# Decay rows stored straight from the sums, later raw weight loads, sums left in PSUM, and another form of the second activation

## Chip, cores and metric

The kernel runs on one core of one Trainium2 chip. The metric is the device time of one execution in microseconds; for the kernel before the median of three runs is taken.

## The reference

Attention with a decay over 4 x 8 heads (576 positions, 64 wide), then two feed-forward layers over the 2304 x 512 result, the second with a slope per inner channel:

```
log_f  = log(clip(f, 1e-4, 1));  cum = cumsum(log_f)
scores = q k^T / sqrt(D) + cum[:, None] - cum[None, :]     # causal
x      = softmax(scores) v
h  = x @ w_in1;  g = h * clip(h + 3, 0, 6) / 6;                 x = g @ w_out1
h  = x @ w_in2;  g = max(h, 0) + alpha * min(h, 0);             out = g @ w_out2
```

## The kernel before

**Attention.** There are 32 heads in 16 pairs. A pair has nine units: four tiles of 128 queries of the first head, one tile with the 64 last queries of both, four tiles of the second head. At step t the loop at L566 issues for unit t the scores (`stage1`, L353), for unit t-1 the maximum (`maxes`, DVE) and the exponentials (`exps`, ACT), for unit t-5 the transposes and their copies, and some steps after a pair the product with v (`stage3`). The order on every engine is the order of issue; nothing is rescheduled.

A score is the sum of two matmuls: L364 (or L376) with the high parts `q1` and `k1`, and L365 (or L378) with `q2` and `k2`. Rows 0 to 63 of those hold low parts, and rows 64 to 67 the decay: two rows with the high and low part of `cum` and two constant rows. For heads 0 and 1 these four rows are written in SBUF (`aug_consts`, `aug_rows`). All the others read them from two DRAM buffers, `aq_d` and `ak_d`, in `prep_head` (L313, L314). The prologue (L467 to L540) computes `cum`, splits it into `hl`, which is a part of the tile `ak`, copies it on POOL into a tile `aq` of the layout of `aq_d`, with constants set by memsets, and stores both tiles. The SP queue issues nearly all DMAs, in order: L520 stores `ak`, L536 stores `aq`, `load_head` brings the raw q and k of a head (608 KB) and, for every second head, the values (320 KB). `prep_head` and `prep_low` make the high and low parts of a head, mostly on POOL; for head 2 they are issued after unit 3.

**Weights.** They come as 64-bit floats and are converted by hand in slices: `fetch` (L113) loads a raw slice of 512 KB into one of two buffers, then ACT takes the magnitude (m), DVE does floor, shift, join and sign (f, s, j, g), and the sign step issues the next fetch. Names and times of these steps are in tables such as `CONV_ATT` (L46), whose numbers are the units after which a step is issued. The first two fetches are issued after unit 2 (L550).

**Layers.** The tokens are three blocks of 768, the inner channels eight groups of 256; a set is one group with one block, 24 sets a layer. A set's product with the first weights is made of seven products of half size (`product`, L689) in three kinds of PSUM bank: P1, P6, P7 and P4 in A (two banks), P2 in B, P5 and P3 in C (one bank each). ACT copies P1, P6 and P5 to SBUF (`keep`); DVE adds P2, P7 and P3 to these copies (`add`, L707); P4 is used in its bank. Each of the four sums is activated in three steps (`activate`, L654): `first` on ACT, `second` on DVE, `third` splits the result into a high part on ACT (L682) and a low part on POOL (L683). The products with the second weights (`piece`, L719) of the set before are put between, in the order of the strings `SEQ`. In layer two `first` makes relu(-h) (L666) and relu(h) (L668), and `second` adds them with the factor -alpha (L677). The tiles `t` of the activation have three buffers, the tiles `s` of the kept products four.

Of the kernel before, what the change touches and what calls it, by code (L numbers as in the profile page):

```python
# [8 lines left out]
F32 = mybir.dt.float32  # L9
I64 = mybir.dt.int64  # L10
U32 = mybir.dt.uint32
F32R = mybir.dt.float32r
BF16 = mybir.dt.bfloat16
AF = mybir.ActivationFunctionType
ALU = mybir.AluOpType
# [6 lines left out]
def decay_attention_ffn2_kernel(ctx, tc, qk, v, f, wi1, wo1, wi2, wo2, alpha, out):  # L22
    nc = tc.nc
    NHEAD = qk.shape[0]
    S = f.shape[1]
# [20 lines left out]
    CONV_ATT = "m0 15 f0 16 s0 17 j0 18 g0 19 m1 24 f1 25 s1 26 j1 27 g1 28 hb 33 lb 35 S1 42 S3 42 S2 44 S4 44 ha 51 la 53 hc 53 lc 60 hd 60 ld 62 m2 69 f2 70 s2 71 j2 72 g2 73 m3 78 f3 79 s3 80 j3 81 g3 82 ho0 78 lo0 80 ho1 87 lo1 89 wi0 90 wi1 93 wo0 99 wo1 102"  # L46
# [231 lines left out]
    def attention():  # L278
        with ExitStack() as ax:
# [196 lines left out]
            aq = pro.tile([NPP, 4, QW], F32R, name="aq")  # L476
            hl = ak[:, 2:4, :]
            nc.gpsimd.memset(zero, 0.0)

# [17 lines left out]
            nc.sync.dma_start(out=alpha_sb, in_=alpha)  # L497
            aug_consts(0)
# [5 lines left out]
            nc.gpsimd.memset(aq.bitcast(F32)[:, :, 512:640], 0.0)  # L504
            nc.gpsimd.memset(aq.bitcast(F32)[:, 2:4, 0:512], -1.0)
# [9 lines left out]
            for a in range(2):  # L515
                nc.gpsimd.memset(aq.bitcast(F32)[32 * a:32 * a + 32, 2:4, 512 + 64 * a:576 + 64 * a], -1.0)
            aug_rows(1)
            load_head(2)
            for a in range(2):
                nc.sync.dma_start(out=ak_d[a, 0:NP], in_=ak[32 * a:32 * a + NP].bitcast(F32))  # L520
            load_head(3)
            prep_head(1)
            prep_low(1)
# [7 lines left out]
            scaled("P", aq[:, 0:2, 0:512], hl[:, :, 0:512].bitcast(F32))  # L531
            for a in range(2):
                ps, t0 = slice(32 * a, 32 * a + 32), 512 + 64 * a
                scaled("P", aq[ps, 0:2, t0:t0 + TAIL], hl[ps, :, 512:S].bitcast(F32))
            for a in range(2):
                nc.sync.dma_start(out=aq_d[a, 0:NP], in_=aq[32 * a:32 * a + NP].bitcast(F32))  # L536
            nc.gpsimd.tensor_scalar(out=alpha_sb, in0=alpha_sb, scalar1=-1.0, scalar2=None, op0=ALU.mult)
# [9 lines left out]
            def aside(t, *fns):  # L547
                side.setdefault(t, []).extend(fns)

            aside(2, lambda: fetch(0), lambda: fetch(1))  # L550
# [60 lines left out]
    P = {}  # L611
# [39 lines left out]
    def aside(d, fn):  # L651
        behind.setdefault(now[0] + int(d), []).append(fn)

    def activate(s, gt, i, n, h, d):  # L654
# [5 lines left out]
        def first():  # L660
            t = P["tp"].tile([128, NB], F32, tag="t", name="t")
            if ff == 0:
                nc.scalar.activation(out=t, in_=h(), func=AF.Relu, bias=three, scale=1.0)
                hold["g"] = t
                return
            nc.scalar.activation(out=t, in_=h(), func=AF.Relu, scale=-1.0)  # L666
            hold["g"] = g32 = P["tp"].tile([128, NB], F32, tag="t", name="t") if (i, n) == (1, 0) else h()
            nc.scalar.activation(out=g32, in_=h(), func=AF.Relu)  # L668
            hold["t"] = t

        def second():
            g32 = hold["g"]
            if ff == 0:
                nc.vector.scalar_tensor_tensor(out=g32, in0=g32, scalar=6.0, in1=h(), op0=ALU.min, op1=ALU.mult)  # L674
            else:
                m = g * FT + i
                nc.vector.scalar_tensor_tensor(out=g32, in0=hold["t"], scalar=alpha_sb[:, m:m + 1], in1=g32,  # L677
                                               op0=ALU.mult, op1=ALU.add)
# [10 lines left out]
    def product(s, c, gt, k):  # L689
# [17 lines left out]
        def add(k2):  # L707
            nc.vector.tensor_add(out=c[k2], in0=h, in1=c[k2])  # L708
# [194 lines left out]
```

## Time and profile before

| | us |
|---|---|
| median of three runs (lowest, highest) | 1015.56 (1013.59, 1016.53) |
| profiled execution | 1012.13 |
| span in its profile | 1010.3 |
| TensorE busy | 965.5 (96%) |
| DVE busy | 735.9 (73%) |
| ACT busy | 589.1 (58%) |
| POOL busy | 590.0 (58%) |

The profile is of one execution. Attention takes the first 219 us of it or so, layer one runs to about 620 us, layer two to the end. A busy TensorE means that its matmuls follow each other without a gap; what other engines do beside it costs nothing until a matmul waits. The waits, the chain of work that ended last, the timeline and the tables by stretch tell where that is.

### The profile page before, as it was taken

The numbers are of one execution on the slowest core, as the hardware profiler recorded it, in microseconds if no ns is written. First come the engines' busy times: TensorE is split into PE (matmuls) and PEld (weight loads), VectorE is DVE, ScalarE is ACT, GpSimd is POOL, SyncE is SP. The second block draws the span as 40 slices with busy tenths as digits, with TensorE's granted clock in tenths as the row PEclk, the third lists the DMA queues.
The fourth block names the chain that finished last, engine by engine and source line by source line (L and its number), as shares of the span: only waits on it lengthen the run. The fifth ranks groups of instructions, "written<-read, shape, count | busy, mean of one in ns | idle before, by whom it ended". The sixth has DMA issues, their size and how long they took to land.

```text
span 1010.3 us, 15919 instructions
## 1 busy us (share of the span) xinstructions
PE 965.5 (96%) x5488; PEld 859.7 (85%) x5488; DVE 735.9 (73%) x1284; ACT 589.1 (58%) x1444; POOL 590.0 (58%) x577
## 2 busy tenths in 40 slices
PE   4999999999999999999999989999999999999998
PEld 3767666678899999998998988789898888898997
DVE  6888988857698788878989846145687788735454
ACT  5677787776555555555654445665565656564452
POOL 8567568956646666566485269566556556532222
PEclk9999999999999999999999999999999999999999
DMA  6555576501424444310576851332344420243531
GB/s 219 174 173 168 176 239 208 150 2 42 156 66 177 178 175 169 107 48 1 198 308 241 308 184 48 137 129 81 125 160 168 166 84 1 104 182 142 229 150 68
DMA packets 36868, 147.57 MB, mean 146 GB/s; under 512 B 4668, under 2 KB 4668, under 8 KB 33652
## 3 DMA queue, kind: packets, MB, share of 16 engines
q1 hardware_dynamic: 36784, 146.56, 41.7%
q8 instruction: 43, 0.70, 0.3%
q14 instruction: 37, 0.30, 0.1%
q10 hardware_dynamic: 4, 0.00, 0.0%
HBM read 98.26 MB, written 44.14 MB: 141 GB/s over the span
## 4 chain that ended last, share of the span: by engine, by line
PE 57%; DVE 23%; POOL 7%; ACT 6%; issue 4%; DMA 2%; SPq 0%; POOLq 0%; ACTq 0%; DVEq 0%
PE o L733 13%; PE hA L700 12%; PE o L731 12%; PE hC L700 7%; PE pv L454 4%; PE hB L700 3%; DVE nm L341 3%; PE tp L397 2%; DVE t L674 2%; PE sc L364 2%; POOL wi L185 2%; POOL g L683 1%; DVE r L751 1%; DVE s L708 1%; ACT g L682 1%
## 5 line engine op out<-in xcount | busy, mean ns | idle before, releaser
L731 PE MATMUL o<-g,wo 128*128 128x384 f32 x1152 | 233.3, 341 | 2.0 <-POOL g L683 2.0
L700 PE MATMUL hA<-xh,wi 128*128 128x384 f32 x768 | 225.8, 339 | 9.0 <-ACT s L705 5.4
L733 PE MATMUL o<-wo,g 128*128 128x512 f32 x864 | 225.5, 395 | 4.0 <-POOL g L683 3.0
L683 POOL TENSOR_TENSOR g<-t,g 128x384 fp32r<-128x384 f32 x120 | 128.8, 1073 | 156.1 <-ACT g L682 134.6
L731 PEld LDWEIGHTS o<-g,wo 128*128 128x128 f32 x1152 | 205.6, 189 | 4.6 <-POOL g L683 3.3
L733 PEld LDWEIGHTS o<-wo,g 128*128 128x128 f32 x864 | 159.8, 188 | 33.2 <-POOL g L683 6.2
L683 POOL TENSOR_TENSOR g<-s,g 128x384 fp32r<-128x384 f32 x72 | 74.7, 1038 | 155.6 <-ACT g L682 153.8
L700 PEld LDWEIGHTS hA<-xh,wi 128*128 128x128 f32 x768 | 142.0, 188 | 15.1 <-ACT s L705 7.6
L751 DVE TENSOR_TENSOR r<-o,r 128x512 f32<-128x512 f32 x126 | 86.2, 687 | 73.8 <-PE o L733 73.7
L700 PE MATMUL hA<-xl,wi 128*128 128x384 f32 x384 | 129.7, 338 | 0.0
L682 ACT CAST g<-t 128x384 fp32r<-128x384 f32 x120 | 61.9, 515 | 113.0 <-DVE t L674 97.3
L700 PE MATMUL hC<-xh,wi 128*128 128x384 f32 x384 | 115.0, 340 | 3.6 <-ACT s L705 3.6
L740 DVE SCALAR_TENSOR_TENSOR r<-o,r 128x384 f32<-128x384 f32 x168 | 90.6, 549 | 21.2 <-PE o L731 21.0
L349 ACT ACTIVATE p<-sc,nm 128x128 f32<-128x128 f32 (+4 forms) x160 | 84.6, 532 | 22.9 <-DVE nm L341 10.9
L245 POOL TENSOR_TENSOR xl<-r,xh 128x384 fp32r<-128x384 f32 x65 | 78.5, 1225 | 4.1 <-ACT xh L240 3.7
L341 DVE TENSOR_REDUCE nm<-sc 128x1 f32<-128x128 f32 (+4 forms) x160 | 71.7, 470 | 10.1 <-PE sc L366 8.5
L700 PEld LDWEIGHTS hC<-xh,wi 128*128 128x128 f32 x384 | 71.3, 189 | 6.7 <-ACT s L705 4.6
L700 PEld LDWEIGHTS hA<-xl,wi 128*128 128x128 f32 x384 | 72.4, 189 | 3.1
L682 ACT CAST g<-s 128x384 fp32r<-128x384 f32 x72 | 37.1, 515 | 60.1 <-DVE s L677 53.4
L397 PE MATMUL tp<-ident,p 128*128 128x128 f32 x384 | 68.6, 282 | 0.6 <-ACT pt L413 0.6
L364 PE MATMUL sc<-k,q 128*128 128x256 f32 (+2 forms) x128 | 55.6, 434 | 11.9 <-DVE k L332 9.8
L700 PE MATMUL hC<-xl,wi 128*128 128x384 f32 x192 | 65.1, 339 | 0.0
(128 smaller groups left out, 1901.8 us busy)
## 6 DMA issues: line engine op xcount, KB each, us to landing
wid<-wi SPq DMA_DIRECT2D x24, 896.0 KB
wi<-wid SPq DMA_DIRECT2D x12, 1792.0 KB
rqk<-in_qk SPq DMA_DIRECT2D x32, 608.0 KB
raw<-in_wi SPq DMA_DIRECT2D x32, 512.0 KB
raw<-in_wo SPq DMA_DIRECT2D x32, 512.0 KB
wod<-wo SPq DMA_DIRECT2D x24, 512.0 KB
wo<-wod SPq DMA_DIRECT2D x12, 1024.0 KB
vt<-in_v SPq DMA_DIRECT2D x16, 320.0 KB
```

The source lines that it names most:

```text
L245: e.tensor_sub(out=XS[k][1][:, b, c], in0=x, in1=XS[k][0][:, b, c].bitcast(F32))
L341: nc.vector.tensor_reduce(out=nm[:, i:i + 1], in_=src, axis=AX.X, op=ALU.max, negate=True)
L349: nc.scalar.activation(out=pt[:, c0:c0 + cw], in_=src, func=AF.Exp, bias=nm[:, 0:1], scale=1.0, accum_out=dsts[i])
L364: nc.tensor.matmul(out=sc[:, 0:n], lhsT=q1[:, qs], rhs=k1[:, 0:n], start=True, stop=False)
L397: nc.tensor.transpose(tp[:, j, :], pt[:, 128 * j:128 * j + 128], ident)
L682: nc.scalar.copy(out=gt[n][i][:, 0], in_=hold["g"])
L683: nc.gpsimd.tensor_sub(out=gt[n][i][:, 1], in0=hold["g"], in1=gt[n][i][:, 0].bitcast(F32))
L700: nc.tensor.matmul(out=h, lhsT=a, rhs=b[:, x, kc], start=new and kc + e == 0, stop=kc == KH - 1 and e == 2, skip_group_check=not new)
L731: nc.tensor.matmul(out=o[:, 0:NB], lhsT=a[:, cs], rhs=b, start=st, stop=sp)
L733: nc.tensor.matmul(out=o, lhsT=b[:, cs], rhs=a, start=st, stop=sp)
L740: later(0, lambda: nc.vector.scalar_tensor_tensor(out=acc, in0=o[:, 0:NB], scalar=1.0 / 6.0, in1=acc, op0=ALU.mult, op1=ALU.add))
L751: nc.vector.tensor_add(out=acc, in0=o, in1=acc)
```

## The change

- In the prologue the tile `aq` holds the constant rows only and has half the size. It is set by one memset and two small ones at the start, and stored early; two small stores put zeros where `cum` has none. The rows of `cum` go from `hl` to `aq_d` by three stores, which are issued after head 2's load and ahead of the `ak_d` stores. The three scalings on POOL and the two old stores are gone.
- `prep_head(1)` and `prep_low(1)` are issued after the constants `three`, `ident` and `maskj`.
- The first two fetches are issued after units 13 and 18 in place of unit 2, and the conversion steps of the first two slices after units 20 to 30 in place of 15 to 28.
- The sums with P2 and P3 are written to their PSUM bank; ACT and DVE read them there, in both layers. The sum with P7 goes to SBUF as before, since its bank goes on to take P4.
- In layer two `second` computes h + (1 - alpha) relu(-h). The relu(h) on ACT and its tile are gone.

```diff
--- before.py
+++ after.py
@@ -43,7 +43,7 @@
     LM, LE, LT, LV = 1, 2, 5, 5
     RD, SD, PA, PB = 3, 6, 7, 9
     DRAIN = {9 * NP + 3: 2, 9 * NP + 4: 2, 9 * NP + 6: 2, 9 * NP + 7: 2}
-    CONV_ATT = "m0 15 f0 16 s0 17 j0 18 g0 19 m1 24 f1 25 s1 26 j1 27 g1 28 hb 33 lb 35 S1 42 S3 42 S2 44 S4 44 ha 51 la 53 hc 53 lc 60 hd 60 ld 62 m2 69 f2 70 s2 71 j2 72 g2 73 m3 78 f3 79 s3 80 j3 81 g3 82 ho0 78 lo0 80 ho1 87 lo1 89 wi0 90 wi1 93 wo0 99 wo1 102"
+    CONV_ATT = "m0 20 f0 21 s0 22 j0 23 g0 24 m1 26 f1 27 s1 28 j1 29 g1 30 hb 34 lb 35 S1 42 S3 42 S2 44 S4 44 ha 51 la 53 hc 53 lc 60 hd 60 ld 62 m2 69 f2 70 s2 71 j2 72 g2 73 m3 78 f3 79 s3 80 j3 81 g3 82 ho0 78 lo0 80 ho1 87 lo1 89 wi0 90 wi1 93 wo0 99 wo1 102"
     CONV_ATT1 = "m0 108 f0 109 s0 110 j0 111 g0 112 m1 117 f1 118 s1 119 j1 120 g1 121 S1 143 S3 145 S2 146 ha 146 hc 146 hb 147 la 147 lc 147 lb 148 S4 149 hd 149 ld 150 m2 150 f2 151 s2 151 j2 152 g2 153"
     CONV_FIRST = "ho0 2 m3 2 lo0 3 f3 3 s3 4 j3 5 g3 6 ho1 8 lo1 9 wi0 30 wi1 33 wo0 36 wo1 38"
     CONV_A = "m0 0 f0 2 s0 3 j0 4 g0 5 m1 4 f1 6 s1 7 j1 8 g1 9"
@@ -473,9 +473,12 @@
             zero = pro.tile([NPP, S], F32, name="zero")
             cum = pro.tile([NPP, S], F32, name="cum")
             ak = pro.tile([NPP, 4, S], F32R, name="ak")
-            aq = pro.tile([NPP, 4, QW], F32R, name="aq")
+            aq = pro.tile([NPP, 2, QW], F32, name="aq")
             hl = ak[:, 2:4, :]
             nc.gpsimd.memset(zero, 0.0)
+            nc.gpsimd.memset(aq, -1.0)
+            for a in range(2):
+                nc.gpsimd.memset(aq[32 * a:32 * a + 32, :, 576 - 64 * a:640 - 64 * a], 0.0)
 
             def aug_consts(a):
                 o0 = 576 - 64 * a
@@ -495,14 +498,16 @@
 
             load_head(1)
             nc.sync.dma_start(out=alpha_sb, in_=alpha)
+            nc.sync.dma_start(out=aq_d.rearrange("a h r c -> (a h) r c")[:, 2:4], in_=aq)
+            for a in range(2):
+                nc.sync.dma_start(out=aq_d[a, :, 0:2, 576 - 64 * a:640 - 64 * a],
+                                  in_=zero[32 * a:32 * a + 32, 0:128].rearrange("p (r c) -> p r c", r=2))
             aug_consts(0)
             aug_consts(1)
             make_identity(nc, identb)
             nc.gpsimd.memset(maskb, 0.0)
             nc.gpsimd.affine_select(out=maskb, in_=maskb, pattern=[[-1, 128]], compare_op=ALU.is_ge,
                                     fill=-1.0e9, base=0, channel_multiplier=1)
-            nc.gpsimd.memset(aq.bitcast(F32)[:, :, 512:640], 0.0)
-            nc.gpsimd.memset(aq.bitcast(F32)[:, 2:4, 0:512], -1.0)
             nc.gpsimd.memset(ak[:, 0:2, :].bitcast(F32), 1.0)
             nc.vector.tensor_scalar(out=fl, in0=fl, scalar1=1e-4, scalar2=1.0, op0=ALU.max, op1=ALU.min)
             nc.scalar.activation(out=fl, in_=fl, func=AF.Ln)
@@ -512,15 +517,15 @@
             nc.vector.tensor_sub(out=hl[:, 1, :], in0=cum, in1=hl[:, 0, :].bitcast(F32))
             aug_rows(0)
             prep_low(0)
-            for a in range(2):
-                nc.gpsimd.memset(aq.bitcast(F32)[32 * a:32 * a + 32, 2:4, 512 + 64 * a:576 + 64 * a], -1.0)
             aug_rows(1)
             load_head(2)
+            nc.sync.dma_start(out=aq_d.rearrange("a h r c -> (a h) r c")[:, 0:2, 0:512], in_=hl[:, :, 0:512].bitcast(F32))
+            for a in range(2):
+                ps, t0 = slice(32 * a, 32 * a + 32), 512 + 64 * a
+                nc.sync.dma_start(out=aq_d[a, :, 0:2, t0:t0 + TAIL], in_=hl[ps, :, 512:S].bitcast(F32))
             for a in range(2):
                 nc.sync.dma_start(out=ak_d[a, 0:NP], in_=ak[32 * a:32 * a + NP].bitcast(F32))
             load_head(3)
-            prep_head(1)
-            prep_low(1)
             nc.gpsimd.memset(three, 3.0)
             make_identity(nc, ident)
             nc.gpsimd.memset(maskj, 0.0)
@@ -528,13 +533,9 @@
                 nc.gpsimd.affine_select(out=maskj[64 * a:64 * a + 64], in_=maskj[64 * a:64 * a + 64],
                                         pattern=[[-1, TAIL]], compare_op=ALU.is_ge,
                                         fill=-1.0e9, base=0, channel_multiplier=1)
-            scaled("P", aq[:, 0:2, 0:512], hl[:, :, 0:512].bitcast(F32))
-            for a in range(2):
-                ps, t0 = slice(32 * a, 32 * a + 32), 512 + 64 * a
-                scaled("P", aq[ps, 0:2, t0:t0 + TAIL], hl[ps, :, 512:S].bitcast(F32))
-            for a in range(2):
-                nc.sync.dma_start(out=aq_d[a, 0:NP], in_=aq[32 * a:32 * a + NP].bitcast(F32))
-            nc.gpsimd.tensor_scalar(out=alpha_sb, in0=alpha_sb, scalar1=-1.0, scalar2=None, op0=ALU.mult)
+            prep_head(1)
+            prep_low(1)
+            nc.gpsimd.tensor_scalar(out=alpha_sb, in0=alpha_sb, scalar1=-1.0, scalar2=1.0, op0=ALU.mult, op1=ALU.add)
             px.close()
             ptp = ax.enter_context(tc.tile_pool(name="ptp", bufs=3, reuse_waits="tile"))
             rcp = ax.enter_context(tc.tile_pool(name="rcp", bufs=1, reuse_waits="tile"))
@@ -547,7 +548,8 @@
             def aside(t, *fns):
                 side.setdefault(t, []).extend(fns)
 
-            aside(2, lambda: fetch(0), lambda: fetch(1))
+            aside(13, lambda: fetch(0))
+            aside(18, lambda: fetch(1))
             ops = conv_ops(0, 0)
             for name, t in table(CONV_ATT):
                 aside(t, ops[name])
@@ -664,9 +666,7 @@
                 hold["g"] = t
                 return
             nc.scalar.activation(out=t, in_=h(), func=AF.Relu, scale=-1.0)
-            hold["g"] = g32 = P["tp"].tile([128, NB], F32, tag="t", name="t") if (i, n) == (1, 0) else h()
-            nc.scalar.activation(out=g32, in_=h(), func=AF.Relu)
-            hold["t"] = t
+            hold["g"] = t
 
         def second():
             g32 = hold["g"]
@@ -674,7 +674,7 @@
                 nc.vector.scalar_tensor_tensor(out=g32, in0=g32, scalar=6.0, in1=h(), op0=ALU.min, op1=ALU.mult)
             else:
                 m = g * FT + i
-                nc.vector.scalar_tensor_tensor(out=g32, in0=hold["t"], scalar=alpha_sb[:, m:m + 1], in1=g32,
+                nc.vector.scalar_tensor_tensor(out=g32, in0=g32, scalar=alpha_sb[:, m:m + 1], in1=h(),
                                                op0=ALU.mult, op1=ALU.add)
 
         def third():
@@ -705,7 +705,9 @@
             nc.scalar.copy(out=c[k], in_=h)
 
         def add(k2):
-            nc.vector.tensor_add(out=c[k2], in0=h, in1=c[k2])
+            got = h if k != 7 else c[k2]
+            nc.vector.tensor_add(out=got, in0=h, in1=c[k2])
+            c[k2] = got
 
         if k in (1, 6, 5):
             at.setdefault(now[0], []).insert(0, keep)
```

## Rows read from the trace of the kernel before

**Rows 1.** TensorE's waits, whole span: us in total, times, longest.

```profile
PE sc L365 <- DMA k<-ak_d: 3.9, 1, 3.9
```

**Rows 2.** Chain of waits, first 30 us: start us, us, what.

```profile
13.23 1.31 POOL aq L92 x2
...
14.56 5.79 DMA aq_d<-aq
...
20.73 4.20 DMA k<-ak_d
```

**Rows 3.** Timeline, first 30 us: start us, us, engine, line, operation, idle before.

```profile
3.35 1.39 DVE L507 TENSOR_SCALAR fl<-fl 64x576 f32<-64x576 f32 x1 [0.18 <-DMA fl<-in_f]
...
8.51 1.43 SPq L491 DMA_DIRECT2D q<-ak  x2
...
9.10 1.79 POOL L332 TENSOR_TENSOR k<-rqk,k 64x576 fp32r<-64x576 f32 x1
9.65 1.91 DVE L333 SCALAR_TENSOR_TENSOR q<-rqk,q 64x640 fp32r<-64x640 f32 x1
...
11.27 0.40 SPq L295 DMA_DIRECT2D rqk<-in_qk  x1
...
11.66 0.55 PE L365 MATMUL sc<-k,q 68*128 68x256 f32 x1 [1.34 <-DVE q L333]
...
13.26 0.46 SPq L295 DMA_DIRECT2D rqk<-in_qk  x1
...
14.75 0.59 PE L376 MATMUL sc<-k,q 128*128 128x288 f32 x1
...
16.34 2.86 SPq L117 DMA_DIRECT2D raw<-in_wi  x2
...
20.83 0.36 PE L364 MATMUL sc<-k,q 128*128 128x256 f32 x1
```

**Rows 4.** Stretches, length us; PE, PEld, DVE, ACT, POOL busy; clock, DMA share, GB/s.

```profile
12.00:14.00 2.00, 2.00 (x9) 1.58 (x9) 1.45 (x5) 0.95 (x4) 1.80 (x4) 1.00 0.84 207
14.00:16.00 2.00, 2.00 (x8) 1.48 (x8) 1.18 (x2) 1.00 (x4) 1.36 (x5) 1.00 1.11 352
16.00:18.00 2.00, 2.00 (x13) 1.76 (x11) 1.29 (x4) 0.92 (x4) 1.92 (x4) 1.00 0.91 312
18.00:20.00 2.00, 2.00 (x16) 1.77 (x15) 1.50 (x4) 2.00 (x9) 1.79 (x1) 1.00 0.97 241
...
26.00:28.00 2.00, 2.00 (x11) 1.69 (x11) 1.45 (x6) 1.29 (x6) 0.20 (x1) 0.50 0.82 279
```

**Rows 5.** The same view, one pair each, with and without conversion.

```profile
44.00:57.20 13.20, 12.52 (x91) 8.48 (x91) 11.80 (x26) 9.26 (x34) 6.06 (x8) 1.00 0.59 178
81.50:93.00 11.50, 11.20 (x89) 8.14 (x88) 9.52 (x22) 9.11 (x36) 8.01 (x9) 1.00 0.57 166
```

**Rows 6.** DVE by form: busy us, mean ns; last row min/median/max.

```profile
L751 DVE TENSOR_TENSOR r<-o,r 128x512 f32<-128x512 f32 x126 | 86.2, 687 | 73.8 <-PE o L733 73.7
L674 DVE SCALAR_TENSOR_TENSOR t<-t,s 128x384 f32<-128x384 f32 x72 | 51.8, 720 | 10.1 <-ACT t L663 9.9
...
L708 DVE TENSOR_TENSOR s<-hC,s 128x384 f32<-128x384 f32 x48 | 26.6, 553 | 39.2 <-PE hC L700 27.2 <-ACT s L705 11.4 <-issue 0.3
...
L674 DVE SCALAR_TENSOR_TENSOR t<-t,hA 128x384 f32<-128x384 f32 x24 | 13.3, 553 | 13.7 <-ACT t L663 13.7
...
L674 DVE SCALAR_TENSOR_TENSOR t<-t,s x72: 544/552/1498, 222.0 to 610.1; 128x384 f32<-128x384 f32 x72
```

**Rows 7.** ACT by form, columns as in the group before.

```profile
L668 ACT ACTIVATE s<-s 128x384 f32<-128x384 f32 x72 | 37.9, 527 | 2.3
```

**Rows 8.** Timeline of TensorE: first and last standstill in the two layers.

```profile
218.78 0.44 PE L700 MATMUL hA<-xh,wi 128*128 128x384 f32 x1 [0.41 <-ACT s L705]
...
873.26 1.19 PE L733 MATMUL o<-wo,g 128*128 128x512 f32 x4 [0.35 <-POOL g L683]
```

**Rows 9.** Chain of waits, the passage between the layers.

```profile
634.50 3.75 POOL wi L185 x3
```

## Prediction, made before the changed kernel was run

> **What bounds the kernel now.** I read TensorE's waits first. Almost all of the span TensorE is busy, so the only time to win is where it stands still. After its first matmul, one wait stands out: 3.9 us for a DMA that brings the decay rows of head 2 [rows 1]. The chain of waits for the first 30 us tells why [rows 2]: POOL scales the decay rows into `aq` from 13.23 on, the store to `aq_d` takes from 14.56 to 20.35, and only then the load of those rows and of `ak_d` may start; it takes 4.20 us and lands at 24.93. The timeline [rows 3] shows what else stands in that queue: on SP the rows of head 3 (issued 13.26) go ahead of the `aq_d` store, and two raw weight blocks of 512 KB (16.34, 2.86 us of issuing for both) go between the store and the loads that the scores wait for. TensorE had done the first half of unit 9's scores by 21.19 (20.83 plus 0.36) and had nothing else. The clock granted over 26 to 28 us, right after that standstill, is 0.50, the lower of the two levels, against 1.00 before it [rows 4].
>
> Attention then runs in pairs of heads, nine units each: 11.5 us where no weight is converted, 13.2 us where four conversion steps lie on DVE [rows 5]. The two layers are TensorE's: the timeline of TensorE lists 22 matmuls between 218 and 874 us with a standstill in front; the first and the last are shown [rows 8]. They sum to 8.6 us up to 549, 7.2 us in the passage from layer one to two (598 to 640) and 2.8 us from 790 on. That, 18.6 us, is all that the two edits in the layers can win.
>
> **Part 1, the decay rows.** Removed: three POOL operations and the store that waits for them. Added: a store of the constant rows and two small ones of zeros, issued early, then three stores straight from `hl`, before the `ak_d` stores. The early three cost SP an issue of some 0.4 to 0.7 us each (0.40 and 0.46 for a head's load, 1.43 for two row copies [rows 3]); they follow the alpha load and end by about 5.5 us, before SP's next work at 8.51, which waits for `hl` anyway. Their 0.36 MB go behind the first loads and take 1.0 us at the 352 GB/s of 14 to 16 us [rows 4]; I take nothing for it, and if the first loads are not through by 7.5 us, the first rows of heads 0 and 1 come up to 1.0 us later.
>
> The late three are issued from about 12.2 us. When do they land? By their shapes, 608 KB of head 2 and 320 KB of values stand ahead of them, and they bring 295 KB. That is 1.25 MB. The DMAs moved 0.41 MB in 12 to 14 us, 0.70 MB in 14 to 16, and then 312 GB/s [rows 4], so 1.25 MB are through at 16.4. Tested on the old order: 2.20 MB stood up to its `aq_d` store; these rates give 19.9, and it landed at 20.35, 0.45 later. So the new store lands near 17, not 20.35. The loads of head 2's rows are then issued at 17.2 to 17.9, behind the `ak_d` stores and head 3 (2.17 MB in all, through at 19.7 by the same rates). The old loads stood behind 3.24 MB; 2.22 of it had gone by 20 us, the rest takes 3.3 us at 312 GB/s, and they landed at 24.93, 1.6 later. With 0.5 to 1.6 us more, then, the new loads land at 20.2 to 21.3. TensorE wants them at 21.19. I keep 0.3 us of the 3.9 as left over: gain 3.6, bounds 1.0 and 3.9.
>
> What is moved past what: on SP the `ak_d` stores and head 3's load go behind three issues, 1.2 to 2.1 us, so head 3 lands about 1 us later than now. Unit 13 wants it about 4.5 us after unit 9, so there is room of about 1 us; if it is gone, POOL's preparation of head 3 is what is late next. On POOL, head 1's two steps go behind `three`, `ident` and `maskj`, which filled POOL from 10.89 (9.10 plus 1.79) to 13.23, 2.3 us [rows 2, 3]; they would end near 13 us against 10.89, and unit 4's matmuls, the first to ask for them, begin at 14.75. The cover is 1.5 to 2 us.
>
> The same move has a small gain at the opening. DVE's clamp of f took 1.39 us, beside a POOL memset that is not there any more, and its step for q of head 0 took 1.91 us beside POOL's step for head 1, which is now later; TensorE waited 1.34 us for it [rows 3]. Bounds 0 and 1.1 us; I take 0.6, nearer the row of the clamp, because the first rows' DMAs follow the clamp and land only a little before. The lower clock after the standstill goes with it: at most 1.0 us by the row of 26 to 28 us, but other engines had caught up during the standstill and TensorE ran through piled-up work, so I take 0.
>
> **Part 2, the raw weights at units 13 and 18.** 1.05 MB leave the queue at 16.3 us; counted above. Their conversion steps now lie in units 20 to 30. Before, 2, 4 and 2 of the eight DVE steps lay in the pairs of units 9 to 17, 18 to 26 and 27 to 35; now 0, 4 and 4. Two pairs differ by 1.7 us for four steps [rows 5], that is 0.4 us per step where DVE has no room. The pair that loses two steps was catching up and would gain little, the pair that wins two pays up to 0.85: I take 0.5 lost, bounds 0 and 0.85. The loads are ahead of their first use by 7 and 8 units, about 9 us, against about 2 us of transfer each, so their waits are hidden; without that cover ACT would stand for up to 3 us.
>
> Prologue and attention together: 3.6 + 0.6 - 0.5 = 3.7 us gained.
>
> **Part 3, sums left in their banks.** Per set, the sums of P2 and P3 stay in PSUM. The banks B and C are next written ten or more steps later (a step is about 1.1 us), so no matmul waits. Layer one's step after it (L674) is shown in both forms: 720 ns on average with both operands in SBUF, 553 ns with one in PSUM. The SBUF form's median is 552, its longest 1498 [rows 6], so the difference is not the operand but the cases in which it is held up; the PSUM form is never held up so. Two steps per set save 2 x 0.167 = 0.33 us of DVE. It counts only where DVE leads the chain: in layer one roughly 222 to 266, 425 to 475 and 484 to 550 us, 160 us or 10 sets of 15.8 us, as the chain of waits reads there: 3.3 us, of 8.6 us of standstill. Against it stands the addition's write into PSUM, which no row shows. Lower bound: 0, as it reads PSUM already (553 ns). Upper: 134 ns, the distance to the 512-wide addition, 687 [rows 6], the nearest row of a heavier DVE operation on PSUM. I take 50 ns, nearer the lower row since the shape is the same: 2 x 10 x 0.05 = 1.0 lost. Layer one: 2.3 us gained, bounds 0.6 and 3.3.
>
> The Trainium skill (Perfetto Trace Analysis, Optimizing Scalar/DVE Operations) speaks against this edit: it puts DVE's access overhead at about 60 ns on SBUF and about 125 ns on PSUM. By that page the two additions and the two steps of a set would each cost 65 ns more, 10 x 4 x 0.065 = 2.6 us as an estimate. On the reading side the two forms of L674 do not agree with it (552 at the median against 553); the writing side is shown by no run here.
>
> **Part 4, layer two's activation.** One ACT operation goes per product, 96 in all, 527 ns in its frequent form [rows 7]. ACT isn't the bound, but each stood between the sum and DVE's step, so g comes 0.53 us sooner. The six standstills from 790 on are waits for g, between 0.34 and 0.72 us; taking 0.53 off each leaves 0.26 of 2.8. As queues are in order, I take 2.0, bounds 0 and 2.8. In the passage at 598 to 640 POOL's queue leads (a run of 3.75 us of low parts [rows 9]); I take 0 there. What is held longer: `t` (three buffers) now lives until POOL's subtraction, as in layer one.
>
> **Sum.** 3.7 + 2.3 + 2.0 = 8.0 us. The profiled execution took 1012.1 us (span 1010.3), so it would be 1004.1; the median of the runs is 3.4 us higher, 1015.6, and becomes 1007.5.
>
> **Rivals.**
> (a) The standstill comes back in another place: each of the three late stores waits for the one ahead, or head 3 lands so late that its preparation is waited for. For it: SP is one queue, and the margin is under 1 us. Against: the byte count above. It gives part 1 about 1.0 in place of 3.6, a sum of 5.4: 1010.2.
> (b) The write into PSUM takes the layers' gain back: 134 ns per addition leaves 0.6 in layer one, and with DVE slower layer two keeps about 0.5. For it: no row shows such a write. Sum 4.8: 1010.8. The Trainium skill's page named above points here.
> (c) Slower: the three `t` buffers of layer two. The fourth activation of a set takes the buffer of the first; ACT must wait until POOL has subtracted it, four steps (4.9 us) later. Where a run of 3.75 us of weights lies in front [rows 9], with about 1 us for the subtraction the edge of 4.9 is reached, and ACT's next copies, which free TensorE's bank, stand behind it. It decides as soon as POOL is over 1 us late in most sets: 1.2 us in each of 12 sets is 14 us lost, net 1021.5. Against: layer one holds `t` in the same way, and its ACT waits there are for DVE.
> (d) More than forecast: the clock's 1.0, all of the opening and most of layer one's 8.6 us, together 13 us: 1002.6.
> (e) No visible effect: DVE paces attention, so that what TensorE wins at 21 us is waited away by unit 35, and the layers stay: 1014.
>
> **Chances.** Forecast (gain 5.5 to 11) 0.56; (a) 0.13; (b) 0.13; (c) 0.05; (d) 0.07; (e) 0.06. About 0.3% (3 us) is what a measurement of this kernel can tell from no change, so faster means under 1012.5. The forecast, (d) and about two thirds of (a) and (b) make faster 0.80; the rest of these and (e) make same 0.15; (c) 0.05. The range 1001.5 to 1013 holds the forecast, (a), (b) and (d)'s middle; it leaves out (c), (e) and the far end of (d).
>
> **What the profile of after would show.** TensorE's wait for `k<-ak_d` near 21 us under 1 us, and the clock at 1.00 there; the `aq_d` stores landing near 17; unit 35's values about 3.7 us earlier; L674 near 553 ns in two forms of three; L708 into hB and hC under 610 ns; no L668; standstills after 790 under 1 us in sum. I would be wrong if ACT's first operation of layer two waits for POOL, if L708 is near 690, or if POOL's k of head 3 stands in front of TensorE.

## The result, and the profile after

| | before | after |
|---|---|---|
| median, us (lowest to highest of four runs each) | 1014.58 (1012.88 to 1016.53) | 1002.22 (1000.51 to 1004.06) |
| profiled execution, us (span) | 1012.13 (1010.3) | 1002.13 (1000.3) |
| busy, us: TensorE, DVE, ACT, POOL | 965.5, 735.9, 589.1, 590.0 | 961.3, 718.3, 539.6, 583.5 |

The ratio of after to before is 0.9878, with an interval of 0.9851 to 0.9905: 12.4 us faster (9.6 to 15.1). The forecast gain was 8.0. The profiled executions differ by 10.0 only, because the profiled one of before is 2.4 us faster than its median.

Both programs issue the same 5488 matmuls in the same order. So the start of the n-th matmul in the one trace can be set against the start of the n-th in the other, each counted from the start of its span. The difference is what after has won by then, and where it changes, time was won or lost:

| matmuls | start in before, us | won in the stretch, us | won by its end, us |
|---|---|---|---|
| 0 to 240, prologue and scores of the first 29 units | 9.8 to 51.9 | 3.8 | 3.8 |
| 240 to 300 | 51.9 to 61.2 | -3.2 | 0.6 |
| 300 to 1440, rest of attention | 61.2 to 218.0 | 1.2 | 1.8 |
| 1440 to 3360, layer one | 218.0 to 567.6 | 3.6 | 5.4 |
| 3360 to 3840, passage | 567.6 to 667.0 | -0.6 | 4.8 |
| 3840 to the last, layer two | 667.0 to 1006.1 | 5.0 | 9.8 |

**Prologue and attention.** TensorE's waits of after from 10 to 72 us (us in total, times, longest) begin so:

```profile
PE sc L378 <- DMA k<-k: 3.3, 1, 3.3
PE sc L364 <- ACT p L349: 2.4, 1, 2.4
```

The wait for `k<-ak_d` of [rows 1] is not there any more, and two others stand in its place. The timeline of after (columns as in [rows 3]) shows the opening, the stores and the second of the two:

```profile
3.63 0.47 DVE L512 TENSOR_SCALAR fl<-fl 64x576 f32<-64x576 f32 x1 [0.47 <-DMA fl<-in_f]
...
8.65 0.82 DVE L333 SCALAR_TENSOR_TENSOR q<-rqk,q 64x640 fp32r<-64x640 f32 x1
...
9.99 0.55 PE L365 MATMUL sc<-k,q 68*128 68x256 f32 x1 [0.67 <-ACT q L88]
...
11.47 0.69 SPq L522 DMA_DIRECT2D aq_d<-ak  x1
12.20 1.70 SPq L525 DMA_DIRECT2D aq_d<-ak  x2
14.00 1.18 SPq L527 DMA_DIRECT2D ak_d<-ak  x2
...
16.16 1.27 SPq L313 DMA_DIRECT2D q<-aq_d  x1
...
17.88 0.24 SPq L314 DMA_DIRECT2D k<-ak_d  x1
...
18.94 0.27 ACT L408 COPY pt<-tp 128x128 f32<-128x128 f32 x1 [4.08 <-DMA q<-aq_d]
...
19.75 0.52 PE L364 MATMUL sc<-k,q 128*128 128x384 f32 x1 [2.42 <-ACT p L349]
...
21.31 0.73 POOL L92 TENSOR_SCALAR q<-rqk 128x640 fp32r<-128x640 f32 x1 [2.74 <-DMA rqk<-in_qk]
```

The clamp and the step for q are short now (0.47 and 0.82 us against 1.39 and 1.91), and the first product that needs q starts at 9.99, not at 11.66. The three late stores are issued from 11.47 on without a wait between them, and the loads that read them from 16.16 on. But ACT's first copy into `pt` stands for 4.08 us; the exponentials queue behind it, their bank stays full, and TensorE stands 2.42 us before the scores of unit 7. The row above puts ACT's wait down to a load, `q<-aq_d`; the chain of waits of after goes through the last store of `ak_d`, which lands at 18.62 (an experiment below decides between them). Later the chain passes through the copy `k<-k`, which brings half of head 7's k:

```profile
14.77 3.85 DMA ak_d<-ak
...
46.16 7.24 DMA k<-k
...
53.53 0.37 PE sc L378
```

SP's own waits from 36 to 66 us and its timeline say why that copy took so long:

```profile
SPq L117 <- DVE wa L153: 3.6, 1, 3.6
```

```profile
43.75 0.36 SPq L117 DMA_DIRECT2D raw<-in_wo  x1
...
44.87 0.72 SPq L295 DMA_DIRECT2D rqk<-in_qk  x1
45.69 0.38 SPq L300 DMA_DIRECT2D vt<-in_v  x1
46.16 0.47 SPq L326 DMA_DIRECT2D k<-k  x1
```

SP stood 3.6 us for a sign step (L153) that has to free a raw buffer; then a raw slice, a head's rows, its values and, behind them, the copy went out within 2.4 us. The stretches show both standstills, the empty queue and the burst (columns as in [rows 4]):

```profile
18.00:20.00 2.00, 0.25 (x1) 0.25 (x2) 0.00 (x0) 1.06 (x5) 0.57 (x1) 1.00 0.76 248
20.00:22.00 2.00, 2.00 (x9) 1.38 (x8) 0.94 (x2) 1.98 (x9) 0.69 (x1) 0.50 0.93 307
...
42.00:44.00 2.00, 1.96 (x15) 1.18 (x15) 2.00 (x6) 1.48 (x6) 2.00 (x2) 1.00 0.01 4
...
48.00:50.00 2.00, 2.00 (x17) 1.51 (x15) 1.82 (x9) 1.99 (x9) 0.01 (x1) 1.00 1.05 351
50.00:52.00 2.00, 0.21 (x2) 0.00 (x0) 2.00 (x5) 0.67 (x2) 1.56 (x2) 1.00 1.03 244
...
54.00:56.00 2.00, 2.00 (x12) 1.84 (x11) 1.64 (x4) 0.42 (x2) 1.21 (x3) 0.53 0.73 183
```

The DMAs moved 4 GB/s while SP stood and 351 behind it. After each standstill the granted clock is at the lower level, 0.50 and 0.53, as it was after the old one [rows 4].

**The layers.** DVE and ACT by form in after (columns as in [rows 6]; L709, L674 and L677 on DVE, L668 on ACT):

```profile
L709 DVE TENSOR_TENSOR hC<-hC,s 128x384 f32<-128x384 f32 x48 | 27.0, 562 | 41.8 <-PE hC L700 30.9 <-ACT s L705 9.1 <-ACT wa L137 1.1
L709 DVE TENSOR_TENSOR hB<-hB,s 128x384 f32<-128x384 f32 x48 | 26.7, 556 | 2.0 <-PE hB L700 1.3 <-ACT s L705 0.7
...
L674 DVE SCALAR_TENSOR_TENSOR t<-t,s 128x384 f32<-128x384 f32 x24 | 18.6, 776 | 4.1 <-ACT t L665 4.0
...
L674 DVE SCALAR_TENSOR_TENSOR t<-t,hA 128x384 f32<-128x384 f32 x24 | 13.3, 553 | 14.2 <-ACT t L665 14.0
...
L674 DVE SCALAR_TENSOR_TENSOR t<-t,hC 128x384 f32<-128x384 f32 x24 | 13.1, 545 | 1.1 <-ACT t L665 1.0
L674 DVE SCALAR_TENSOR_TENSOR t<-t,hB 128x384 f32<-128x384 f32 x24 | 13.1, 545 | 2.8 <-ACT t L665 2.8
...
L668 ACT ACTIVATE t<-hC 128x384 f32<-128x384 f32 x24 | 11.8, 491 | 39.0 <-DVE hC L709 38.9
```

An addition into the bank takes 562 ns in hC, where the one into SBUF took 553 [rows 6], and 556 in hB, where it took 549. The activation step that reads its sum in a bank takes 545 ns.

In layer two the waits of TensorE's weight loads (PEld) from 640 us on, first of before, then of after, are these:

```profile
PEld o L733 <- POOL g L683: 4.5, 7, 1.2
PEld o L733 <- ACT g L682: 2.0, 4, 0.9
```

```profile
PEld o L735 <- POOL g L683: 0.3, 1, 0.3
```

Before, the loads waited 6.5 us for g; after, 0.3. I had read only the waits of the matmuls [rows 8]. In the passage, the chain of waits of after has these two pieces:

```profile
576.66 8.25 DMA fd<-wa
...
629.69 3.75 POOL wi L185 x3
```

POOL's run of low parts is as long as in [rows 9], and a transfer of 8.25 us through DRAM stands in front. Nothing was won there.

### The profile page after: what moved, and what is told of

Its sections match the earlier page's. It is cut to its first block, busy times and chain, and to the rows that moved or that the text cites. A ratio compares the mean times of both kernels' runs of the same rounds, so it can differ in the third digit from the quotient of the medians.

```text
span 1000.3 us, 15853 instructions
## 1 busy us (share of the span) xinstructions
PE 961.3 (96%) x5488; PEld 860.7 (86%) x5488; DVE 718.3 (72%) x1284; ACT 539.6 (54%) x1348; POOL 583.5 (58%) x573
## 4 chain that ended last, share of the span: by engine, by line
PE 70%; DVE 14%; POOL 4%; ACT 4%; issue 3%; DMA 3%; SPq 1%; ACTq 0%; DVEq 0%; POOLq 0%
PE o L735 20%; PE hA L700 15%; PE o L733 12%; PE hC L700 8%; PE pv L454 4%; PE hB L700 4%; PE tp L397 3%; DVE nm L341 2%; PE sc L364 2%; DVE t L674 2%; DVE r L742 1%; PE sc L365 1%; POOL g L683 1%; DMA raw<-in_wo 1%; DVE nm L343 1%
## 5 line engine op out<-in xcount | busy, mean ns | idle before, releaser
L683 POOL TENSOR_TENSOR g<-t,g 128x384 fp32r<-128x384 f32 x192 | 201.8, 1052 | 305.9 <-ACT g L682 285.1
L682 ACT CAST g<-t 128x384 fp32r<-128x384 f32 x192 | 98.6, 514 | 193.9 <-DVE t L677 94.9
L705 ACT COPY s<-hA 128x384 f32<-128x384 f32 x96 | 45.7, 476 | 31.9 <-PE hA L700 31.7
L700 PE MATMUL hB<-xh,wi 128*128 128x384 f32 x192 | 57.1, 338 | 0.0
```

Of the source, the lines that this page charges most:

```text
L682: nc.scalar.copy(out=gt[n][i][:, 0], in_=hold["g"])
L683: nc.gpsimd.tensor_sub(out=gt[n][i][:, 1], in0=hold["g"], in1=gt[n][i][:, 0].bitcast(F32))
L700: nc.tensor.matmul(out=h, lhsT=a, rhs=b[:, x, kc], start=new and kc + e == 0, stop=kc == KH - 1 and e == 2, skip_group_check=not new)
```

## The experiments

Gains are against the kernel before. Those at a matmul come from the profiled execution, as in the table above; the medians are of all runs of a kernel.

| kernel | median, us (runs) | ratio (interval) | won by matmul 240, 480, 1440, 3360, 3840, last |
|---|---|---|---|
| e1_prologue_alone | 1010.27 (5) | 0.9956 (0.9939 to 0.9973) | 3.6, 0.9, -0.5, -0.2, -0.6, -0.4 |
| e2_sums_layer_one | 1009.74 (8) | 0.9955 (0.9943 to 0.9967) | -1.3, -1.2, -0.8, 3.1, 3.0, 3.0 |
| e3_activation_alone | 1009.25 (4) | 0.9947 (0.9933 to 0.9962) | -1.7, -2.0, -0.6, -0.6, -1.8, 3.1 |
| after | 1002.22 (4) | 0.9878 (0.9851 to 0.9905) | 3.8, 1.0, 1.8, 5.4, 4.8, 9.8 |
| e4_early_fetch | 1002.78 (4) | 0.9886 (0.9869 to 0.9903) | -0.9, -0.4, 0.3, 3.6, 4.3, 9.4 |
| e5_ak_first | 1003.54 (6) | 0.9895 (0.9871 to 0.9918) | 3.6, 0.4, 0.2, 4.1, 4.6, 9.6 |
| e6_fetch_apart | 999.45 (4) | 0.9863 (0.9843 to 0.9882) | 2.9, 4.3, 3.3, 7.7, 7.7, 12.8 |
| e7_both | 999.24 (4) | 0.9857 (0.9834 to 0.988) | 2.6, 3.5, 2.8, 6.4, 6.6, 11.6 |
| e8_ak_behind_aq | 998.56 (4) | 0.9846 (0.983 to 0.9861) | 3.6, 4.4, 3.4, 6.6, 6.7, 11.8 |
| e9_swap_only | 1002.55 (5) | 0.9885 (0.9868 to 0.9902) | 2.8, -0.6, -0.8, 3.1, 4.4, 9.4 |

The kernel before had a median of 1014.07 to 1014.59 beside them. e2 and e3 have the old prologue, and yet they stand up to 2.0 us behind in attention: single executions differ there by that much. A gain of a layer is therefore read as the difference of two columns.

### One part alone on the kernel before

e1 has the prologue's part and the later fetches; e2 leaves the sums of P2 and P3 in their banks in layer one only; e3 changes the second activation only. The cores of the three edits, in this order, against before:

```diff
+            nc.sync.dma_start(out=aq_d.rearrange("a h r c -> (a h) r c")[:, 0:2, 0:512], in_=hl[:, :, 0:512].bitcast(F32))
...
-            aside(2, lambda: fetch(0), lambda: fetch(1))
+            aside(13, lambda: fetch(0))
+            aside(18, lambda: fetch(1))
```

```diff
-            nc.vector.tensor_add(out=c[k2], in0=h, in1=c[k2])
+            got = h if k != 7 and s[0] == 0 else c[k2]
+            nc.vector.tensor_add(out=got, in0=h, in1=c[k2])
+            c[k2] = got
```

```diff
-            hold["g"] = g32 = P["tp"].tile([128, NB], F32, tag="t", name="t") if (i, n) == (1, 0) else h()
-            nc.scalar.activation(out=g32, in_=h(), func=AF.Relu)
-            hold["t"] = t
+            hold["g"] = t
```

> The kernel before with parts 1 and 2 alone (decay rows from the sums, later fetches). If each part's gain lies in its own stage, attention ends 1.8 us sooner than before, as in the changed kernel, with the same standstill of 2.4 us near 19.7 us and of 3.3 us near 50 us, the layers give nothing more, and the time is 1.8 us under the one before (ratio 0.998). If the loss near 50 us was an accident of one execution, attention ends 4 to 5 us sooner and the ratio is 0.995.

> The kernel before with the sums of P2 and P3 left in their banks in layer one alone. If DVE's relief is what layer one won, the prologue is as before, TensorE is 3.0 to 3.6 us ahead near 565 us, the passage takes 0.6 of it back, and the time falls by 3 us (ratio 0.997). If layer one won by the shifted arrival of its weights and not by the sums, it falls by less than 1 us.

> The kernel before with the new activation of layer two alone; the sums go to SBUF. If the removed ACT operation is what layer two won, TensorE gains 4 to 5 us between 740 and 880 us, and its weight loads wait for g under 1 us there where they waited 6.5 (ratio 0.995). If DVE's relief through the banks is what counts, DVE's steps stay near 660 ns and the gain is 2.5 us or less (0.9975). If ACT waits for the three t buffers, the time is longer than before.

**e1** is 4.3 us faster by the medians (2.7 to 6.2 by the interval). Its profiled execution is the slowest of its five, 1012.39, and keeps nothing: 3.6 us won by matmul 240 are down to 0.9 at matmul 480. The wait is that of after (TensorE's waits of e1, 10 to 72 us):

```profile
PE sc L378 <- DMA k<-k: 3.2, 1, 3.2
```

So this standstill belongs to the prologue's part and the moved fetches, not to the edits in the layers. The standstill is that of the first expectation, the time that of the second; where the faster executions win their time is not shown, since one alone was profiled.

**e2** wins 3.8 us in layer one (from -0.8 to 3.1) and nothing in layer two; there its weight loads still wait for g:

```profile
PEld o L735 <- POOL g L683: 5.0, 8, 1.2
PEld o L735 <- ACT g L682: 1.4, 2, 0.7
```

Within one program, its additions into hC take 561 ns in layer one and those out of hC into SBUF 554 in layer two: the write into the bank costs 7 ns.

**e3** wins 4.9 us in layer two (from -1.8 to 3.1), as much as after (5.0), and the waits of its weight loads for g from 640 us on are down to one:

```profile
PEld o L731 <- POOL g L681: 0.4, 1, 0.4
```

Its DVE step did not get faster in the form with two SBUF operands (678 ns against 664 before). So layer two's gain is that of the ACT operation that is gone, and the sums left in their banks add nothing measurable to it (5.0 in after, 5.0 to 5.1 in e4 to e9). The three parts alone give 4.3 + 4.9 + 5.3 = 14.5 us by the medians, together 12.4: within the intervals they add up.

### The fetches back at unit 2

e4 is after with the first two fetches at unit 2 and the old times of the first two slices in `CONV_ATT`:

```diff
-            aside(13, lambda: fetch(0))
-            aside(18, lambda: fetch(1))
+            aside(2, lambda: fetch(0), lambda: fetch(1))
```

> The changed kernel with part 2 undone: both raw blocks are fetched at unit 2 again and converted at units 15 to 28. If the loss near 50 us comes from the later fetches (SP stands 3.6 us for the sign step, and head loads, a raw block and the copy of head 7's k go out together), that standstill of 3.3 us is gone, unit 9 starts at most 1 us later than in the changed kernel, attention ends 4 to 5 us sooner than before and the time is 2 to 3 us under the changed kernel's. If the denser conversion steps on DVE are the loss, as the prediction had it, the gain is 0.5 us; if the raw blocks still hold up head 2's rows, unit 9 waits 3 us or more and the time is longer than the changed kernel's.

Measured: 1002.78, the same as after; none of the three expectations holds as a whole. The standstill for `k<-k` does not appear, but unit 9 waits for its decay rows again (TensorE's waits, then the chain of waits):

```profile
PE sc L365 <- DMA k<-ak_d: 2.0, 1, 2.0
```

```profile
18.72 7.07 DMA k<-ak_d
```

Behind two raw slices the load takes 7.07 us. So the later fetches do keep the queue free for these rows, as the forecast said, but they pay for it at 50 us; as made, part 2 shifts a standstill and wins nothing that the times show.

### Which store the copy into pt waits for

My reading of the 4.08 us was that `pt` takes the memory of `ak`, whose pool has been closed, so that its first writer waits for the last store that reads `ak`. If so, a change in the order of the stores changes which one is named, and another place for `ak` takes the wait away. e5 stores `ak_d` ahead of `aq_d`, e9 allocates `ak` behind `aq`, each against after:

```diff
             load_head(2)
+            for a in range(2):
+                nc.sync.dma_start(out=ak_d[a, 0:NP], in_=ak[32 * a:32 * a + NP].bitcast(F32))
             nc.sync.dma_start(out=aq_d.rearrange("a h r c -> (a h) r c")[:, 0:2, 0:512], in_=hl[:, :, 0:512].bitcast(F32))
...
-            for a in range(2):
-                nc.sync.dma_start(out=ak_d[a, 0:NP], in_=ak[32 * a:32 * a + NP].bitcast(F32))
             load_head(3)
```

```diff
-            ak = pro.tile([NPP, 4, S], F32R, name="ak")
             aq = pro.tile([NPP, 2, QW], F32, name="aq")
+            ak = pro.tile([NPP, 4, S], F32R, name="ak")
```

> The changed kernel with the two ak_d stores issued ahead of the three aq_d stores. In the changed kernel ACT's first copy into pt stands 4.1 us until 18.94, and TensorE 2.4 us in front of unit 7's scores. If that is because pt lies in the memory of ak and must wait until the ak_d stores have read it, ACT's copy starts by 17 us, TensorE's standstill there falls under 0.8 us, unit 9 starts 1.5 to 2.4 us sooner and the time falls by about 2 us unless the standstill near 50 us takes it back (a loss there of 3.3 to 5 us). If the copy waits for the aq_d stores or for the loads of head 2's rows, it starts at 18.5 us or later and nothing is gained.

> The changed kernel with that allocation alone; the fetches stay with the sign steps. If the standstill near 20 us and the one near 50 us are in series, it gains 1 to 2.4 us at 25 us and keeps the one near 50 us, whose loss may take it back: 1000 to 1002 us. If removing the first makes the second longer by the same amount (the copy of head 7's k lands at a time set by SP and the DMAs alone), attention ends where it does in the changed kernel, 1002 us.

ACT's first copy into `pt`, in the timelines of e5 and of e9:

```profile
18.47 0.27 ACT L408 COPY pt<-tp 128x128 f32<-128x128 f32 x1 [3.52 <-DMA aq_d<-ak]
```

```profile
16.16 0.27 ACT L408 COPY pt<-tp 128x128 f32<-128x128 f32 x1 [0.99 <-POOL k L92]
```

In e5 the copy is no sooner and waits for the `aq_d` store, now the last to read `ak`. That alone would also fit a wait for `aq_d` whatever the order. In e9 the order of after is kept, and the copy starts 2.8 us earlier than in after and waits for no DMA; the 0.99 us before it stood there in before too. The two together show the cause of this standstill: the copy needs the memory of `ak`. The time does not follow: 1003.54 and 1002.55 against 1002.22. In e9 POOL waits longer for head 3's rows (3.14 us, until 21.91), unit 9 waits 1.4 us for `k<-ak_d`, and the standstill for `k<-k` is 2.4 us long.

### The fetches of slices 2 and 3 apart from the sign steps

e6 is after with the fetches of slices 2 and 3 taken out of the sign steps and issued after units 28 and 37; e7 has e5's order of the stores besides, e8 e9's place for `ak`. First e6 against after, then what e7 and e8 add to it:

```diff
-            fetch(wseq.index((ff, g, s)) + 2)
+            if (ff, g, s) not in ((0, 0, 0), (0, 0, 1)):
+                fetch(wseq.index((ff, g, s)) + 2)
...
             aside(18, lambda: fetch(1))
+            aside(28, lambda: fetch(2))
+            aside(37, lambda: fetch(3))
```

```diff
             load_head(2)
+            for a in range(2):
+                nc.sync.dma_start(out=ak_d[a, 0:NP], in_=ak[32 * a:32 * a + NP].bitcast(F32))
```

```diff
-            ak = pro.tile([NPP, 4, S], F32R, name="ak")
             aq = pro.tile([NPP, 2, QW], F32, name="aq")
+            ak = pro.tile([NPP, 4, S], F32R, name="ak")
```

> The changed kernel with the third and fourth raw blocks fetched at units 28 and 37, apart from the sign steps at units 24 and 30. If the standstill near 50 us comes from SP waiting 3.6 us for the sign step with head loads queued behind it, so that the copy of head 7's k lands 7.2 us after its issue, then SP has no wait for a sign step there, the copy lands in under 5 us, the standstill of 3.3 us is gone, attention ends about 3 us sooner than in the changed kernel and the time falls by 2 to 3 us. If the dense conversion steps on DVE set the pace in units 20 to 35, the standstill goes but attention gains under 1 us.

> Both edits of the two runs before. If the two standstills are separate causes in series, attention ends 4.5 to 5.5 us sooner than in the changed kernel and the time is about 997.5 us. If the first only shifts the same work towards the second, or DVE paces units 9 to 35, it is no better than the better of the two.

> The kernel with the raw fetches apart (units 28 and 37), and in the prologue the tile ak allocated behind aq, so that the first pt tile lies over tiles whose reads ended long before and not over ak. If ACT's first copy into pt waits for the last store that reads ak, whichever that is, the copy now starts by 16.5 us in place of 18.5 to 19, TensorE's standstill of 1.4 to 2.4 us in front of unit 7 falls under 0.5 us, and attention ends 1 to 2.4 us sooner than with the fetches apart alone: 997 to 998.5 us. If the copy's wait is for something else, or the second pt tile waits for the same stores with the same price at unit 4's copies, nothing changes (999.5 us).

**e6** is 14.6 us faster than before by the medians (12.0 to 15.9 by the interval), its median 2.8 below that of after, and what it wins at the start stays: 4.3 us at matmul 480, 3.3 at attention's end. SP has no wait for a sign step from 30 to 70 us, and of TensorE's wait for `k<-k` this is left:

```profile
PE sc L379 <- DMA k<-k: 0.6, 1, 0.6
```

The copy leaves later than in after, but with the raw slice behind it (SP's timeline of e6):

```profile
46.98 0.47 SPq L327 DMA_DIRECT2D k<-k  x1
47.55 0.53 SPq L117 DMA_DIRECT2D raw<-in_wo  x1
```

In the seven traces without the burst this copy lands 3.6 to 4.5 us after its issue, in after, e1, e5 and e9 6.5 to 7.8. From matmul 240 to 300 these four lose 3.0 to 3.7 us; e4, e6, e7 and e8 lose nothing there.

**e7** has the same time, 999.24. **e8**, at 998.56 the lowest median of all, can't be told from e6. The copy into `pt` starts at 15.85 (the 0.99 us before it, as long as in before, are put down to the `aq_d` store), and unit 7 does not stand; TensorE's waits and the chain of waits show what is late next:

```profile
PE sc L366 <- DMA k<-ak_d: 1.6, 1, 1.6
```

```profile
14.82 6.16 DMA rqk<-in_qk
...
21.84 1.88 POOL k L92 x2
```

The rows of head 2 come 1.6 us late, and head 3's load and POOL's preparation of it lead the chain; at matmul 60 e8 is 4.2 us ahead and e6 1.6, by matmul 240 3.6 and 2.9.

The four kernels of the whole change in which the fetches of slices 2 and 3 hang on the sign steps (after, e4, e5, e9) have medians of 1002.2 to 1003.5 and overlap in their runs. The three with those fetches apart have medians of 998.6 to 999.5, and each of their runs is below all runs of after; e5, measured beside e6 and e7, has one run of six below theirs, 997.88, and five above. Among the things tried in the prologue, this is the one that moved the time.

## Why the prediction was right, and where it was not

The time lies in the range, 5.3 us below the predicted one: 1.0 of that is the kernel before, whose median was 1014.6 in these runs, and 4.4 are gain that I did not forecast. The profiled pair shows 9.8 us by the last matmul: the two layers have 4.3 more than I forecast, prologue, attention and passage 2.5 less; the other 2.6 of the 12.4 are placed by no trace. By its own steps:

**Decay rows, 3.6 of the sum: the mechanism right, its gain moved on.** The load that waits for the stores is issued at 16.16 (17.2 to 17.9 forecast), and by matmul 240 3.8 us are won (2.8 to 3.8 in after, e1, e5 and e9), against 3.7 forecast for the end of attention. That after does not wait for these rows near 21 us is luck: its unit 9 comes to them at 23.54 only, held up by the new standstill. In e8 and e9, which do not have that, TensorE asks for them at about 20.1 and 20.8 and gets them at 21.71 and 22.22. I had them landing at 20.2 to 21.3 and left TensorE's wish at 21.19, although I forecast an earlier opening; the wait that is left is 1.6 and 1.4 us, not 0.3. What failed besides is the list of what waits for SP's queue. I moved the `ak_d` stores behind three issues and asked only for head 3; I did not ask which memory they read and who takes it next. So ACT stands 4.08 us and TensorE 2.42 (the cause is shown by e5 and e9). In this program the new wait decides nothing by itself: where e8 and e9 take it away, head 3 and the rows of head 2 are late in its place.

**Opening, 0.6:** the first matmul starts 1.0 us earlier and the first product with q 1.67 (11.66 to 9.99), more than the bound of 1.1. The eight traces with the new prologue start their first matmul at 8.8 us; of the old one, before and e3 start at 9.8 and e2 at 11.2. So the term is 1.0 or more, and one execution does not size it.

**Moved conversions, -0.5 with a bound of -0.85: the step that failed.** I priced four steps on DVE and wrote that the loads are early enough for their first use. The sign step also issues the next fetch on SP, in front of a head's rows, its values and the copy of its k. SP stood for sign steps before the change as well, 3.3 and 2.6 us between 30 and 70 us, without harm to TensorE; moved to units 24 and 30 it stood 3.6 us in front of loads that were due, and 3.2 us went from matmul 240 to 300. e6 shows it: the same kernel with the fetches apart keeps them. The cost that I did price does not show: e6, e7 and e8 have the same steps in units 20 to 30 and win 0.8 to 1.4 us from matmul 240 to 480. Prologue and attention, 3.7 forecast, came to 4.3 (2.7 to 6.2) in e1's medians, but to 1.8, -0.5, 0.2 and -0.8 in the profiled executions of after, e1, e5 and e9; against e2 and e3, which are 0.6 to 0.8 us behind before at that place, that is 0.8 more at most. The traces thus do not bear the 3.7 out.

**Layer one, 2.3 forecast, 3.6 in after and 3.8 in e2.** The saving on DVE was sized about right: L674 took 51.8 + 13.3 = 65.1 us before and 18.6 + 13.3 + 13.1 + 13.1 = 58.1 after, 0.29 us per set where I had 0.33. The cost that I set against it was not: 7 to 9 ns per addition in place of 50, 0.2 us in ten sets in place of 1.0. That alone would have made it 3.1; with the saving as measured, too, ten sets give 2.7. The Trainium skill (Perfetto Trace Analysis, Optimizing Scalar/DVE Operations) gives DVE an access overhead of about 60 ns on SBUF and 125 on PSUM; the 65 ns between them, the estimate of the prediction, are seen here on neither side: 562 against 553 ns for the write, 545 to 553 against a median of 552 for the read. The gain comes in the three stretches that I had named: after wins 0.9 us by 266 us, 1.2 more at 457 to 463 and 1.7 from there to 546. But it is more than I could see, because I summed the wrong waits. TensorE's matmuls from 1440 to 3240 stand 8.1 us in before and 6.8 in after, 1.4 less, while 3.8 are won in that stretch. The waits of its weight loads there sum to 14.3 and 14.7 us in e1 and e3, which leave layer one as it was, and to 10.6 and 10.8 in e2 and after: 3.5 to 4.1 less. In before they sum to 13.2, since its clock was lower for a while. Here are the weight load that ends the first long standstill and the stretch behind it, in before and in e1, and the same weight load in after:

```profile
243.25 0.19 PEld L700 LDWEIGHTS hA<-xh,wi 128*128 128x128 f32 x1 [2.42 <-DVE s L708]
```

```profile
244.00:248.00 4.00, 4.00 (x16) 4.00 (x15) 3.72 (x6) 2.29 (x6) 1.72 (x2) 0.60 0.00 0
```

```profile
243.75 0.19 PEld L702 LDWEIGHTS hA<-xh,wi 128*128 128x128 f32 x1 [2.44 <-DVE s L710]
```

```profile
244.00:248.00 4.00, 3.61 (x20) 3.16 (x19) 3.72 (x7) 2.29 (x6) 2.02 (x2) 1.00 0.00 0
```

```profile
240.57 0.19 PEld L700 LDWEIGHTS hA<-xh,wi 128*128 128x128 f32 x1 [1.62 <-DVE s L709]
```

After the same standstill the clock is 0.60 in before and 1.00 in e1, and in e3 as well. The lower clock cost before 1.5 us in 20 matmuls, but its next waits were shorter for it: by matmul 1672 e1 and e3 stand where before does (0.02 us ahead). So the clock gave none of the 3.8 us; e4, e5 and e8, whose clock is lower once in layer one, win 3.2 to 3.9 there too. Why the gain is 3.8 and not 2.7 stays open.

**Layer two, 2.0 with a bound of 2.8, measured 5.0 and 4.9 (e3).** The mechanism was right, the size was not, and the bound was no bound. In the second product g is the operand that is loaded, so a late g shows at the weight load; the wait of the matmul behind it shows what is left over. I summed the latter, 2.8 us; the former was 6.5.

**Passage, 0:** -0.6 in the profiled execution; the traces of the experiments range from -1.3 to 1.2 there, so this says nothing.

**Rivals.** (a): its first half is wrong, the stores do not wait for one another. Its second was half right: POOL waits 2.74 us for head 3 in after, without harm to TensorE while others are later. The standstill did come back elsewhere, in two places that (a) does not name. (b) is refuted by the 7 to 9 ns. (c): ACT's first operation of layer two (L668) waits for the sums and, in its rows, never for POOL; layer two is faster. (d), 1002.6, hit the time with another sum: neither the prologue's clock nor all of the standstill, but layer two. (e) is refuted in the layers by e2 and e3, and in attention by e6 to e8, which keep 2.8 to 3.4 us to its end.

**What the profile should have shown:** the wait near 21 us (not there, by luck as said), L674, the additions under 610 ns (556 and 562) and no standstill after 790 came out. Two signs did not. Unit 35's values came 0.5 to 1.0 us earlier and not 3.7, since the standstill of 3.3 us lies in front of them. The clock near 21 us is 0.50, not 1.00, behind the new standstill at 18 to 20 us.

## What to carry to other kernels

A step that is moved takes along the transfers that it issues and the memory that its transfers read: list for each queue what stands behind its next wait, and for each store who writes next into the tile that it reads. Bound the gain from a late operand by the waits of the instruction that takes it, weight loads as well as matmuls. When a wait is removed, look first at how much of the gain is left ten, thirty and a hundred microseconds later, by the start of the same matmul in both traces. And before a gain is put down to the clock, look for a trace that has the same wait at another clock.

## What the runs showed of the hardware that was not expected

An addition that writes its result to PSUM costs 7 to 9 ns more than the same to SBUF (562 and 561 against 553 and 554 ns). An activation step of layer one with an operand in a bank is not held up (545 to 553 ns on average in after, no longer than 556 in 72 instances, 40 of which start while POOL runs an instruction), while the form with two SBUF operands ranges from 544 to 1368, and to 1498 in before. The traces show with what: all 24 of its instances over 600 ns in before, and all 10 in after, start while a POOL instruction is running and end 0.41 to 0.42 us after that one ends; no instance that starts beside an idle POOL takes more than 560. One pair in before:

```profile
241.02 1.30 POOL L245 TENSOR_TENSOR xl<-r,xh 128x384 fp32r<-128x384 f32 x1
241.39 1.34 DVE L674 SCALAR_TENSOR_TENSOR t<-t,s 128x384 f32<-128x384 f32 x1
```

So what DVE wins by the sums left in their banks is that two of its four steps per set no longer wait for POOL. The granted clock went to the lower level behind standstills of 2.4 us (0.50 at 20 to 22 us in after, 0.60 at 244 to 248 in before), and stayed at 1.00 behind the same standstill of 2.4 us in e1 and e3: a standstill of that length does not decide it by itself.
